# Attention: values stationary on halves of the array's columns, row sums from the exponentials, the second gate in four steps

## The chip, the cores and the metric

The program runs on one core of a Trainium2 chip. The metric is the device time of one execution in microseconds (us). The kernel before was timed three times: 1039.23 us in the median, from 1036.54 to 1039.69. Its engines, as the profile names them, are PE (TensorE, the matmuls; PEld is its weight loads), DVE (VectorE), ACT (ScalarE), POOL (GpSimd) and SP (the queue that issues most DMAs).

## What is computed

Three stages follow one another; each needs the whole result of the one before.

```python
# 1. attention: 2 batches, 8 heads, 576 rows, head size 64, a window of 128 keys
scores = where(0 <= rel < 128, q @ k.T / 8 + bias, -1e9)
attn   = exp(scores - max(scores));  attn /= attn.sum(-1) + 1e-9
x      = attn @ v                       # 1152 rows of 8 * 64 = 512
# 2. eight experts, each row goes to its best one (capacity 288)
e = argmax(x @ w_gate);  x = gate_w * (relu(x @ w1[e]) @ w2[e])
# 3. eight dense experts, mixed by a balanced matrix
P = exp(x @ w_gate2 - max);  8 times: rows, then columns of P to equal sums
out = sum over e of P[:, e] * (relu(x @ u1[e]) @ u2[e])
```

## The kernel before

**Attention.** The 576 rows of a batch are cut into blocks of at most 128, ten in all; blocks 4 and 9 have 64 rows. A unit is a block with four of the eight heads, so there are 20 units, and unit u belongs to block u // 2. A block looks at its own keys and at those of the block before it in its batch, so most units have two key parts, and the first block of a batch has one. Each unit passes through these steps:

- `scores` (PE, L444 and L437): the heads lie in pairs on the two halves of the array's rows (64 rows each).
- `pick` and `limit` (DVE, L453 and L470): mask, bias and the row's maximum; `powers` (ACT, L479): the exponential of one head at a time.
- `turn_p` (PE, L488) turns the probabilities, and `take_p` (ACT L501 and L508, POOL L509, DVE L506) copies them to `pT`, split by key part.
- `values` (PE, L532, and L522 for blocks of 64 rows): the turned probabilities are the stationary operand (128 columns), the values stream. `vb` holds 64 value columns and a column of ones for each head, so the row sum comes out as column 65. A matmul streams 128 columns (`WIDE`), more than the 65 that are used. In float32 each matmul is two records in the trace.
- `norm` (DVE, in three steps: L557, L559, L561, or L546, L548, L552 for 64 rows): row sum plus 1e-9, reciprocal, product into `x`. The result of `values` has a single PSUM bank (`xps`), so `values` of the next unit waits for the last step of `norm`.

When both units of a block are normed, `turn_x` (L569), `take_x`, `logits` (L583), `top`, `gate` and the counting steps choose each row's expert. Casts that split weights in two parts (`split_hi` on ACT L215, `split_lo` on POOL and DVE L222) are strewn in between.

The order of all this is written out by hand: the table `ORDER` names the steps, and the function `in_order` makes every engine run its instructions in that order. No engine overtakes in its own queue.

**First experts.** From about 108.6 us on, eight experts in turn: two layers in split precision (L772, L776).

**Second experts.** The first of the eight dense experts goes in three chunks of 384 rows (`j`). Into its layer 1 (L1301) and layer 2 (L1340) the steps of the list `sink` are mixed by `sink_next`: `gate_2` first, one step with three rounds of eight matmuls (L1074), a copy out of PSUM (`lsb`, DVE L1078), three transposes (L1081) and another copy (L1082); then eight rounds of row sums and column sums (the column sums with a matmul on PE, L1111). In this part the instructions are not in a table's order: the compile step places them, and token sums (`tsums`, L1184 to L1212) for the later experts stand among them. The other seven experts then run in passes with fewer products (L1383, L1414), up to the end.

Of the kernel before, what the change touches and what calls it, by code (L numbers as in the profile page):

```python
# [1 line left out]

# [7 lines left out]
F32 = mybir.dt.float32  # L10
# [19 lines left out]
take_q.0 load_block.2 scores.0 load_v.0 limit.0.1 turn_q.1 load_block.4 constants take_k.1 take_q.1 rest_k.1  # L30
limit.0.0 turn_k.2 turn_q.2 load_block.3 limit.0.1 load_weight.0 limit.0.0 more_constants powers.0.1 rest_q.1
powers.0.0 scores.1 turn_p.0.1 turn_p.0.0 take_k.2 limit.1.0 take_q.2 limit.1.0 scores.2 take_p.0.0 limit.1.1 sides
rest_q.2 zero_row powers.1.0 take_p.0.1 limit.1.1 pick.2.0 pick.2.1 values.0.0 turn_p.1.0 limit.2.0 values.0.1
rest_k.2 limit.2.0 turn_k.4 norm.0 take_k.4 limit.2.1 limit.2.1 powers.1.1 norm.0 turn_p.1.1 powers.2.0 scores.3
turn_p.2.0 rest_k.4 norm.0 turn_k.3 turn_q.3 pick.3.0 limit.3.0 limit.3.0 scores.4 load_v.1 powers.2.1 take_p.1.0
take_k.3 values.1.0 load_weight.1 pick.3.1 take_p.2.0 take_p.1.1 powers.3.0 limit.3.1 rest_k.3 turn_p.2.1 limit.3.1
split_hi.0 split_lo.0 split_hi.1 split_hi.2 values.1.1 split_hi.3 turn_q.4 pick.4.0 limit.4.0 split_lo.1 turn_p.3.0
split_lo.2 split_lo.3 limit.4.0 powers.4.0 norm.1 norm.1 scores.5 norm.1 take_p.2.1 pick.4.1 values.2.1 pick.5.1
take_p.3.0 load_weight.2 load_v.2 take_q.3 turn_x.0 limit.5.1 take_q.4 limit.4.1 rest_q.3 powers.3.1 load_block.5
take_x.0 values.2.0 load_weight.3 split_hi.4 limit.4.1 turn_p.3.1 norm.2 limit.5.1 split_lo.4 split_hi.5 pick.5.0  # L40
split_lo.5 norm.2 logits.0 split_hi.6 take_p.3.1 split_hi.7 turn_p.4.0 scores.6 top.0 norm.2 powers.5.1 limit.5.0
top.0 values.3.0 limit.5.0 pick.6.1 rest_q.4 take_p.4.0 split_hi.8 limit.6.1 pick.6.0 turn_p.5.1 values.3.1
limit.6.1 top.0 powers.4.1 norm.3 split_lo.6 turn_p.4.1 load_block.6 split_hi.9 split_hi.10 norm.3 scores.7
limit.6.0 split_hi.11 turn_k.5 norm.3 values.4.0 take_p.5.1 powers.5.0 turn_p.5.0 choice.0 pick.7.0 take_p.4.1
pick.7.1 limit.6.0 split_lo.7 values.4.1 limit.7.1 turn_q.5 gate.0 powers.6.1 take_p.5.0 turn_p.6.1 limit.7.1 norm.4
take_k.5 powers.6.0 take_q.5 scores.8 choice.0 norm.4 norm.4 turn_x.1 pick.8.0 take_p.6.1 limit.8.0 limit.7.0
limit.7.0 take_x.1 values.5.1 turn_p.6.0 load_v.3 values.5.0 turn_k.6 rows pick.8.1 limit.8.0 norm.5 logits.1
rest_k.5 take_k.6 top.1 count.0 norm.5 powers.7.0 take_p.6.0 norm.5 scores.9 pick.9.0 rest_k.6 powers.8.0 turn_x.2
# [41 lines left out]
def fused_kernel(ctx, tc, q, k, v, wg1, w1, w2, wg2, u1, u2, out, capacity):  # L90
# [157 lines left out]
    with ExitStack() as st:  # L248
# [225 lines left out]
        def powers(a):  # L474
# [3 lines left out]
            for a in range(2 * i, 2 * i + 2):  # L478
                nc.scalar.activation(pr[:n, a, :], sc[:n, a, :], AF.Exp, bias=nmx[:n, a:a + 1], scale=-1.0)  # L479
# [1000 lines left out]
```

## Time and profile before

| | |
|---|---|
| median of three runs | 1039.23 us |
| the profiled execution, its own time | 1038.18 us |
| its span from first to last instruction | 1036.1 us |
| PE busy over the span | 1018.7 us (98%) |
| DVE / ACT / POOL busy | 677.8 / 387.3 / 315.5 us |
| mean granted clock of PE, as a share of 2.4 GHz | 0.998 |
| attention, up to the first matmul of the experts | 0 to 108.6 us |
| first experts | 108.6 to 264 us |
| second experts | 264 to 1036 us |

A busy time counts an instruction from its start to its end. Matmuls are pipelined, so several are in flight at once; how long a group of them holds PE is read from the start of the group to the start of the next. A wait is idle time of an engine, put down to what ended it.

### The profile page before, as it was taken

Reading aid. Unit: us, or ns where it says so; the run is one execution under the profiler, and the core shown is the slowest. Engines: PE = TensorE matmul, PEld = TensorE weight load, DVE = VectorE, ACT = ScalarE, POOL = GpSimd, SP = SyncE. Lnnn points to the kernel's source line nnn. Section 1 sums busy time; section 2 is a strip of 40 time slices with the busy share of each in tenths; the row PEclk is TensorE's granted clock in tenths of the full one; section 3 lists DMA queues with packets and bytes.
Section 4 is the critical chain, followed back from the end, with each engine's and each line's share of the span. In section 5 each row is a group of like instructions: output and inputs, shape, how many; then the busy total and the mean of one; then the engine's idle time right before and its main releaser. Section 6 shows DMA issues by size and latency. Waiting matters only on the chain.

```text
span 1036.1 us, 16836 instructions
## 1 busy us (share of the span) xinstructions
PE 1018.7 (98%) x6388; PEld 930.3 (90%) x6388; DVE 677.8 (65%) x1644; ACT 387.3 (37%) x838; POOL 315.5 (30%) x305
## 2 busy tenths in 40 slices
PE   8999999999999999999999999999999999999997
PEld 6888999999889998999898999999898999999896
DVE  7988788778783347575756657575756657575752
ACT  6744477767321313232332323232322323232320
POOL 6533153341200123341313332241313332242113
PEclk9999999999999999999999999999999999999999
DMA  9931589986200112020211112020211112020102
GB/s 216 230 71 58 168 213 249 248 255 215 79 1 1 49 34 81 2 82 6 78 41 41 41 41 83 1 82 1 82 41 42 41 41 82 1 82 1 41 1 92
DMA packets 74103, 83.22 MB, mean 80 GB/s; under 512 B 31585, under 2 KB 45921, under 8 KB 74018
## 3 DMA queue, kind: packets, MB, share of 16 engines
q1 hardware_dynamic: 71906, 76.59, 25.0%
q0 software_dynamic: 2112, 5.52, 2.0%
q8 instruction: 51, 0.84, 0.3%
q14 instruction: 34, 0.28, 0.1%
HBM read 77.37 MB, written 4.73 MB: 79 GB/s over the span
## 4 chain that ended last, share of the span: by engine, by line
PE 72%; issue 2%; POOL 1%; DVE 1%; POOLq 0%; ACT 0%
PE pr L1414 31%; PE pr L1383 30%; PE ops L1340 5%; PE hps L1301 5%; PE pb L772 1%; POOL out_dram L1418 1%; PE pb L776 1%; PE lps L1074 0%; DVE tsums L1187 0%; POOL w_wlo L1278 0%; PE cps L1111 0%; POOLq L1476 0%; DVE lsb L1078 0%; DVE y_lo L1184 0%; PE ltp L1081 0%
## 5 line engine op out<-in xcount | busy, mean ns | idle before, releaser
L1414 PE MATMUL pr<-w_whi,hT 128*128 128x512 f32 x1008 | 315.8, 390 | 0.2 <-DVE hT L1375 0.2
L1414 PEld LDWEIGHTS pr<-w_whi,hT 128*128 128x128 f32 x1008 | 189.2, 188 | 39.5 <-DVE hT L1375 0.5
L1414 PE MATMUL pr<-w_wlo,hT 128*128 128x512 f32 x504 | 196.4, 390 | 0.0
L1278 POOL TENSOR_TENSOR w_wlo<-r,w_whi 128x512 fp32r<-128x512 f32 x56 | 71.4, 1294 | 290.4 <-ACT w_whi L1277 180.5
L1416 DVE SCALAR_TENSOR_TENSOR acc<-pr,Pm,acc 128x512 f32<-128x512 f32 x126 | 91.3, 745 | 89.0 <-PE pr L1414 88.7
L1374 ACT ACTIVATE hT<-pr 128x256 fp32r<-128x256 f32 (+1 forms) x168 | 69.0, 411 | 176.0 <-DVE pr L1391 176.0
L1375 DVE SCALAR_TENSOR_TENSOR hT<-pr,hT 128x256 fp32r<-128x256 f32 (+1 forms) x168 | 77.0, 458 | 80.1 <-ACT hT L1374 80.1
L1383 PE MATMUL pr<-y_hi,wy 128*128 128x320 f32 (+1 forms) x560 | 122.7, 297 | 0.0
L1414 PEld LDWEIGHTS pr<-w_wlo,hT 128*128 128x128 f32 x504 | 94.6, 188 | 19.5 <-POOL w_wlo L1278 0.5
L1383 PEld LDWEIGHTS pr<-y_hi,wy 128*128 128x128 f32 x560 | 93.8, 188 | 0.3 <-DVE hT L1375 0.3
L1271 POOL TENSOR_TENSOR wy<-r,wy 128x512 fp32r<-128x512 f32 x28 | 40.0, 1427 | 172.1 <-ACT wy L1270 172.1
L1383 PE MATMUL pr<-y_lo,wy 128*128 128x256 f32 (+1 forms) x280 | 83.3, 297 | 0.0
L191 DVE TENSOR_TENSOR wlo<-w,whi 128x1024 fp32r<-128x1024 f32 x66 | 80.7, 1225 | 3.1 <-issue 3.1
L179 ACT CAST whi<-w 128x1024 fp32r<-128x1024 f32 x66 | 69.1, 1051 | 19.5 <-DMA w<-in_moe_w_dram 15.3
L772 PE MATMUL pb<-h,whi 128*128 128x384 f32 x256 | 74.9, 361 | 0.4 <-DVE t L792 0.4
L772 PE MATMUL pb<-xt,whi 128*128 128x384 f32 x256 | 74.3, 362 | 0.6 <-PEq L946 0.3
L1277 ACT CAST w_whi<-r 128x512 fp32r<-128x512 f32 x56 | 33.1, 619 | 94.1 <-PE pr L1414 93.2
L1374 ACT ACTIVATE hT<-h 128x256 fp32r<-128x256 f32 (+1 forms) x56 | 24.9, 445 | 115.7 <-DVE h L1391 115.7
L1383 PE MATMUL pr<-y_hi,wx_wlo 128*128 128x256 f32 (+1 forms) x224 | 64.6, 288 | 0.0
L1383 PE MATMUL pr<-y_hi,wx_whi 128*128 128x256 f32 (+1 forms) x224 | 64.4, 288 | 0.0
L1383 PE MATMUL pr<-y_lo,wx_whi 128*128 128x256 f32 (+1 forms) x224 | 64.4, 287 | 0.0
L1255 POOL TENSOR_TENSOR sums<-r 128x512 f32<-128x512 f32 x28 | 37.0, 1324 | 80.8 <-DMA r<-in_moe_w_dram 45.6
(363 smaller groups left out, 2253.6 us busy)
## 6 DMA issues: line engine op xcount, KB each, us to landing
w<-in_moe_w_dram SPq DMA_DIRECT2D x36, 1024.0 KB, 6.9
r<-in_moe_w_dram SPq DMA_DIRECT2D x56, 512.0 KB, 3.9
kb<-in_k_dram SPq DMA_DIRECT2D x8, 256.0 KB, 4.0
qb<-in_q_dram SPq DMA_DIRECT2D x8, 256.0 KB, 4.7
vb<-in_v_dram SPq DMA_DIRECT2D x8, 256.0 KB, 6.9
xg_d<-xg SPq DMA_DIRECT2D x8, 256.0 KB, 2.3
kb<-in_k_dram SPq DMA_DIRECT2D x2, 128.0 KB, 4.1
qb<-in_q_dram SPq DMA_DIRECT2D x2, 128.0 KB, 3.6
```

The source lines that it names most:

```text
L179: nc.scalar.copy(his[i][:, sl, :], raws[i][:, sl, :])
L191: nc.vector.tensor_tensor(out=los[i][:, sl, :], in0=raws[i][:, sl, :], in1=his[i][:, sl, :].bitcast(F32), op=ALU.subtract)
L772: nc.tensor.matmul(ps[:, 0:2 * W], whi, x.rearrange("p r w -> p (r w)"), start=(m == 0), stop=(m == K - 1))
L1271: nc.gpsimd.tensor_tensor(out=wy[1][:, i], in0=x, in1=wy[0][:, i].bitcast(F32), op=ALU.subtract)
L1278: nc.gpsimd.tensor_tensor(out=w2p[1][:, k], in0=x, in1=w2p[0][:, k].bitcast(F32), op=ALU.subtract)
L1301: nc.tensor.matmul(hpss[f], a, bb[c][:, cols], start=(c == 0 and m == 0), stop=(c == ND - 1 and m == 2))
L1340: nc.tensor.matmul(ops, a[:, tcol], bb, start=(m == 0), stop=(m == 3 * NF - 1))
L1374: nc.scalar.activation(hi, src, AF.Relu)
L1375: nc.vector.scalar_tensor_tensor(out=lo, in0=src, scalar=0.0, in1=hi.bitcast(F32), op0=ALU.max, op1=ALU.subtract)
L1383: nc.tensor.matmul(ps, a[:, i, c, f], b, start=(c == 0 and m == 0), stop=(c == 1 and m == 2))
L1414: nc.tensor.matmul(ops, a[:, k, s * P:(s + 1) * P], b[:, k, :], start=(m == 0), stop=(m == 6 * QP - 1))
L1416: nc.vector.scalar_tensor_tensor(out=acc[s], in0=ops, scalar=Pm[:, s, e:e + 1], in1=acc[s], op0=ALU.mult, op1=ALU.add)
```

## The change

The diff touches three places.

1. **Attention.** The values of two heads are stationary, each on one half of the array's columns (64 columns, `tile_position=(0, j * D)`), and the turned probabilities stream through. The result is turned (head size on the partitions), so two steps are new: `take_v` copies it from PSUM on ACT, and `turn_v` turns it back on PE with two transposes, into the other half of the same bank. The row sums are no longer a 65th column: they come from `accum_out` of the exponentials, one more ACT instruction for each of the 80. Column of ones, padding to 128 columns and the special form for 64 rows are gone.
2. **Second gate.** One step with three rounds becomes four steps: matmuls of round 0; turn of round 0 and matmuls of round 1; turn of 1 and matmuls of 2; turn of 2 and the start of the balancing. The copy `lsb` goes from DVE to ACT; the copy after the turn and the final sum become one reduction on DVE.
3. **Second chunk of the first dense expert.** Each block of layer 1 is cut in two, with one step of `sink` between the halves.

```diff
@@ ORDER
-limit.9.0 limit.9.1 take_x.2 take_q.6 top.1 values.6.1 limit.8.1 turn_p.7.0 rest_q.6 gate.1 scores.10 choice.1
...
+values.6.1 limit.8.1 take_v.6 turn_p.7.0 rest_q.6 gate.1 scores.10 turn_v.6 choice.1 take_p.7.1 logits.2 load_weight.4
...
@@ load_v
-            vb[t] = la.tile([P, H, D + 1], F32, tag="vb", name=f"vb{t}", bufs=4)
-            nc.sync.dma_start(out=vb[t][:n, :, 0:D], in_=v[b, :, s:s + n, :].rearrange("h p d -> p h d"))
-            nc.gpsimd.memset(vb[t][:, :, D:D + 1], 1.0)
+            vb[t] = la.tile([P, H, D], F32, tag="vb", name=f"vb{t}", bufs=4)
+            nc.sync.dma_start(out=vb[t][:n], in_=v[b, :, s:s + n, :].rearrange("h p d -> p h d"))
@@ powers
-                nc.scalar.activation(pr[:n, a, :], sc[:n, a, :], AF.Exp, bias=nmx[:n, a:a + 1], scale=-1.0)
+                nc.scalar.activation(pr[:n, a, :], sc[:n, a, :], AF.Exp, bias=nmx[:n, a:a + 1], scale=-1.0,
+                                     accum_out=sums_of[u][:n, a:a + 1])
@@ values, and two new steps
-            for j in range(2):
-                h = head(g, i2, j)
-                at = h * (D + 1)
-                cols = min(WIDE, (H - h) * (D + 1))
-                for i, (tk, nk) in enumerate(kparts[t]):
-                    nc.tensor.matmul(xpd[u][:n, i2, j * (D + 1):j * (D + 1) + cols], pTd[u, i2][:nk, i, j, :n],
-                                     vb[tk].rearrange("p h d -> p (h d)")[:nk, at:at + cols],
-                                     start=(i == 0), stop=(i == len(kparts[t]) - 1))
+                xpd[u] = ps_x.tile([P, 4, P], F32, tag="xps", name="xps")
+            for i, (tk, nk) in enumerate(kparts[t]):
+                for j in range(2):
+                    nc.tensor.matmul(xpd[u][j * D:(j + 1) * D, i2, :n], vb[tk][:nk, head(g, i2, j), :],
+                                     pTd[u, i2][:nk, i, j, :n], start=(i == 0), stop=(i == len(kparts[t]) - 1),
+                                     tile_position=(0, j * D))
+
+        def take_v(u):
+            n = blocks[units[u][0]][2]
+            xvd[u] = wk.tile([P, 2, P], F32, tag="xv", name="xv", bufs=1)
+            nc.scalar.copy(xvd[u][:, :, :n], xpd[u][:, 0:2, :n])
+
+        def turn_v(u):
+            n = blocks[units[u][0]][2]
+            for i in range(2):
+                nc.tensor.transpose(xpd[u][:n, 2 + i, :], xvd[u][:, i, :n], ident)
@@ norm
-            nc.vector.tensor_scalar_add(rec[:n], xps[:, :, :, D:D + 1], EPS)
+            rec = sums_of[u]
+            nc.vector.tensor_scalar_add(rec[:n], rec[:n], EPS)
...
-                                    in0=xps[:, :, :, 0:D], in1=rec[:n].to_broadcast([n, 2, 2, D]), op=ALU.mult)
+                                    in0=xpd[u][:n, 2:4, :].rearrange("p i (j d) -> p i j d", j=2),
+                                    in1=rec[:n].rearrange("p (i j o) -> p i j o", i=2, o=1).to_broadcast([n, 2, 2, D]),
+                                    op=ALU.mult)
@@ gate_2, now called with j
-            lsb = tp.tile([P, CH], F32, tag="t1", name="lsb")[:2 * E]
-            nc.vector.tensor_copy(lsb, lps[:2 * E, :])
+        lsbs[j] = tp.tile([P, CH], F32, tag="t1", name="lsb")[:2 * E]
+        nc.scalar.copy(lsbs[j], lps[:2 * E, :])
+    def turn_2(j):
+        ltp = ps_k.tile([P, CH], F32, tag="pk", name="ltp")
+        for i in range(TPC):
+            nc.tensor.transpose(ltp[:, i * 2 * E:(i + 1) * 2 * E], lsbs[j][:, i * P:(i + 1) * P], ident[:2 * E, :2 * E])
+        nc.vector.tensor_reduce(out=lg2[:, j * TPC:(j + 1) * TPC],
+                                in_=ltp[:, :TPC * 2 * E].rearrange("p (s r e) -> p s e r", s=TPC, e=E), op=ALU.add, axis=AX.X)
-    sink = [gate_2, None, sinkhorn_start] + [sinkhorn_rows, None, sinkhorn_columns] * 8
+    sink = [partial(gate_2, 0), both_2(0), both_2(1), last_2, None, None] + [sinkhorn_rows, None, sinkhorn_columns] * 8
@@ second chunk of the first dense expert
+            if j == 1:
+                layer1(f, range(2))
+                sink_next()
             layer1(f, range(2, ND) if f in hpss else range(ND))
```

Three places show what moves. The first is PE at the change from block 3 to block 4; `sps` are scores, `ptp` turned probabilities, `xps` the bank of `values`, `xtp` the turned rows of a whole block. Before:

```order
L532 MATMUL xps<-vb_499,pT 128x128
L532 MATMUL xps<-vb_743,pT 128x128
L488 MATMUL ptp<-ident,pr 128x64 x4
L488 MATMUL ptp<-ident,pr 128x128 x2
L444 MATMUL sps<-kS,qT_829 128x256 x12
L569 MATMUL xtp<-ident,x 128x128 x4
L522 MATMUL xps<-vb_743,pT 128x130
```

Now, with `turn_v` as L534 and `values` as L521:

```order
L521 MATMUL xps<-pT,vb_503 64x128 x2
L521 MATMUL xps<-pT,vb_759 64x128 x2
L491 MATMUL ptp<-ident,pr 128x64 x4
L491 MATMUL ptp<-ident,pr 128x128 x2
L445 MATMUL sps<-kS,qT_848 128x256 x12
L534 MATMUL xps<-ident,xv 128x128 x2
L556 MATMUL xtp<-ident,x 128x128 x4
L521 MATMUL xps<-pT,vb_759 64x64 x2
```

The two new transposes stand right ahead of `xtp`, which reads the rows that DVE makes from them. The second place is ACT while the first weights are split (`whi`), in the third microsecond decade. Before:

```order
L479 ACTIVATE pr<-sc,nmx 128x128 x2
L575 COPY xT<-xtp 128x512
L215 CAST whi_529<-w_1_418 128x512 x4
L479 ACTIVATE pr<-sc,nmx 128x128 x2
L508 COPY pT<-ptp 128x256
L215 CAST whi_594<-w_2_497 128x512
```

Now, with `take_v` as L528:

```order
L481 ACTIVATE pr,rec<-sc,nmx 128x128 x2
L562 COPY xT<-xtp 128x512
L217 CAST whi_538<-w_1_420 128x512
L528 COPY xv<-xps 128x256
L217 CAST whi_538<-w_1_420 128x512 x3
L481 ACTIVATE pr,rec<-sc,nmx 128x128 x2
L508 COPY pT<-ptp 128x256
L217 CAST whi_601<-w_2_501 128x512
```

One copy is new between the casts, and each exponential now also writes a row sum (`rec`). The third place is the second gate's copy `lsb`. Before it was on DVE, here its third round among the token sums:

```order
L1184 TENSOR_TENSOR y_lo_1975<-tsums,y_hi_1971 128x256
L1187 TENSOR_TENSOR tsums<-y_hi_1973,y_lo_1977 128x256
L1187 TENSOR_TENSOR tsums<-y_hi_1972,y_lo_1976 128x256
L1078 COPY lsb<-lps 16x384
L1204 TENSOR_TENSOR tsums<-tsums 128x256
```

Now it is on ACT, with the second and the third round shown:

```order
L1314 ACTIVATE h__5673<-hps_5660 128x384
L1066 COPY lsb<-lps 16x384
L1183 CAST y_hi_2049<-tsums 128x256
L1183 CAST t_0_5592<-tsums 128x256
L1314 ACTIVATE h__5708<-hps_5695 128x384
L1183 CAST y_hi_2051<-tsums 128x256
L1066 COPY lsb<-lps 16x384
```

The third copy left a queue of token sums on DVE and stands behind three casts of token sums on ACT.

## Rows read from the trace of the kernel before

**Rows 1.** Busy time by stage: stage and length, then PE, PEld, DVE, ACT, POOL.
```profile
20.00:33.00 13.00, 12.02 (x108) 10.18 (x107) 11.05 (x52) 12.02 (x32) 11.51 (x12) 1.00 1.00 291
33.00:60.00 27.00, 25.41 (x231) 22.07 (x231) 24.29 (x143) 14.93 (x44) 9.26 (x15) 1.00 0.78 179
60.00:92.00 32.00, 31.20 (x318) 28.16 (x317) 30.22 (x173) 16.65 (x53) 12.86 (x16) 1.00 0.17 51
92.00:108.60 16.60, 16.14 (x120) 13.44 (x119) 12.86 (x74) 4.85 (x16) 3.20 (x4) 1.00 0.20 65
```
**Rows 2.** Waits of PE over the whole span: who for whom, us, times, longest.
```profile
PE ltp L1081 <- DVE lsb L1078: 2.1, 1, 2.1
...
PE xps L532 <- DVE x L561: 0.6, 2, 0.4
```
**Rows 3.** PE in order of time: start, us, line, operation, records.
```profile
52.71 1.65 PE L522 MATMUL xps<-vb,pT 128*128 128x130 f32 x8
54.29 0.44 PE L488 MATMUL ptp<-ident,pr 128*128 128x128 f32 x2
...
76.49 1.06 PE L532 MATMUL xps<-vb,pT 128*128 128x128 f32 x8
77.38 0.60 PE L569 MATMUL xtp<-ident,x 128*128 128x128 f32 x4
77.82 1.06 PE L532 MATMUL xps<-vb,pT 128*128 128x128 f32 x8
...
79.56 0.97 PE L444 MATMUL sps<-kS,qT 64*128 64x256 f32 x12
80.47 1.15 PE L583 MATMUL lgp<-wg_sb,xT 128*128 128x120 f32 x8
```
**Rows 4.** PE by line in attention: records, busy us, mean ns, idle before.
```profile
L532 PE MATMUL xps<-vb,pT 128*128 128x128 f32 (+1 forms) x224 | 31.1, 279 | 2.0 <-DVE pT L506 0.6 <-DVE x L561 0.6 <-PE sps L444 0.5
...
L522 PE MATMUL xps<-vb,pT 128*128 128x130 f32 (+1 forms) x32 | 6.8, 319 | 0.2 <-DVE x L552 0.2
```
**Rows 5.** Weight loads by shape: of 128 columns and of 64 columns.
```profile
L444 PEld LDWEIGHTS sps<-kS,qT 64*128 64x128 f32 x144 | 9.3, 185 | 2.0 <-issue 1.2 <-DVE rec L557 0.2 <-DVE nmx L470 0.2
...
L444 PEld LDWEIGHTS sps<-kS,qT 64*64 64x64 f32 x48 | 2.3, 131 | 0.2 <-DVE rec L557 0.2
```
**Rows 6.** ACT in order of time.
```profile
23.35 0.35 ACT L508 COPY pT<-ptp 128x256 f32<-128x256 f32 x1
...
31.75 0.21 ACT L607 ACTIVATION_READ_ACCUMULATOR ex<-lgp,ngm 128x1 f32 x1
31.84 0.70 ACT L479 ACTIVATE pr<-sc,nmx 128x128 f32<-128x128 f32 x2
```
**Rows 7.** DVE by line, the steps of norm: records, busy us, mean ns.
```profile
L561 DVE TENSOR_TENSOR x<-xps,rec 128x256 f32<-128x256 f32 x16 | 6.7, 416 | 0.3
...
L552 DVE TENSOR_TENSOR x<-xps,rec 64x128 f32<-64x128 f32 x8 | 2.3, 287 | 0.2
...
L546 DVE TENSOR_SCALAR rec<-xps 64x2 f32<-64x2 f32 x8 | 1.3, 158 | 3.6 <-PE xps L522 3.5
```
**Rows 8.** PE in order of time at the third turn of the second gate.
```profile
278.70 0.34 PE L1301 MATMUL hps<-y_hi,wlo 128*128 128x384 f32 x1
278.88 0.33 PE L1301 MATMUL hps<-y_hi,whi 128*128 128x384 f32 x1
281.30 0.35 PE L1081 MATMUL ltp<-ident,lsb 16*128 16x16 f32 x3 [2.08 <-DVE lsb L1078]
```
**Rows 9.** DVE in order of time at the same place.
```profile
277.87 2.92 DVE L1187 TENSOR_TENSOR tsums<-y_hi,y_lo 128x256 f32<-128x256 f32 x2
280.71 0.54 DVE L1078 COPY lsb<-lps 16x384 f32<-16x384 f32 x1
```
**Rows 10.** PE by single microseconds: busy, records, granted clock, DMA.
```profile
109.00:110.00 1.00, 1.00 (x8) 0.69 0.00 0
...
112.00:113.00 1.00, 1.00 (x7) 0.60 1.04 408
```

More of the change, by code (lines that the diff above doesn't have):

```diff
@@ L39 @@
[L39 to L48, printed above, removed]
@@ new lines @@
+take_v.5 turn_k.6 rows pick.8.1 limit.8.0 norm.5 logits.1 turn_v.5 rest_k.5 take_k.6 top.1 count.0 norm.5 powers.7.0
+take_p.6.0 norm.5 scores.9 pick.9.0 rest_k.6 powers.8.0 turn_x.2 pick.9.1 limit.9.0 limit.8.1 load_block.7 turn_q.6
+place.0 limit.9.1 powers.7.1 choice.0 top.1 turn_p.7.1 limit.9.0 limit.9.1 take_x.2 take_q.6 top.1 values.6.0
+values.6.1 limit.8.1 take_v.6 turn_p.7.0 rest_q.6 gate.1 scores.10 turn_v.6 choice.1 take_p.7.1 logits.2 load_weight.4
+norm.6 choice.1 load_v.5 limit.10.0 limit.10.0 load_v.4 count.1 limit.10.1 powers.9.1 scale_x.0 turn_q.7 limit.10.1
@@ new lines @@
+powers.8.1 norm.6 choice.1 place.1 scores.11 top.2 norm.6 limit.11.0 take_p.7.0 powers.9.0 top.2 powers.10.0 take_q.7
+turn_p.8.0 limit.11.1 limit.11.0 gate.2 load_block.9 rest_q.7 turn_p.8.1 turn_k.7 take_p.8.1 take_k.7 top.2 values.7.1
+values.7.0 norm.7 norm.7 scale_x.1 load_v.8 take_p.8.0 take_v.7 turn_p.9.0 turn_p.9.1 turn_p.10.0 take_p.9.0 scores.12
+turn_v.7 norm.7 powers.10.1 turn_x.3 values.8.1 values.8.0 take_v.8 turn_p.10.1 choice.2 take_p.9.1 take_x.3 pick.12.1
+logits.3 turn_v.8 limit.12.1 rest_k.7 mark.0 norm.8 norm.8 limit.11.1 norm.8 count.2 take_p.10.0 pick.12.0 top.3 top.3
@@ new lines @@
+limit.12.1 limit.12.0 table.0 add_table.0 place.2 values.9.0 values.9.1 powers.11.1 take_p.10.1 norm.9 choice.2
+limit.12.0 top.3 take_v.9 turn_p.11.1 powers.11.0 scores.13 turn_v.9 take_p.11.1 norm.9 norm.9 load_block.8 turn_x.4
+turn_p.11.0 mark.1 take_x.4 choice.2 choice.3 pick.13.0 gate.3 take_p.11.0 powers.12.1 values.10.0 values.10.1
+load_v.6 pick.13.1 limit.13.0 table.1 take_v.10 logits.4 turn_v.10 limit.13.0 norm.10 limit.13.1 count.3 add_table.1
+scale_x.2 turn_k.8 norm.10 norm.10 turn_p.12.1 powers.12.0 split_lo.8 limit.13.1 turn_p.12.0 values.11.1 values.11.0
@@ new lines @@
+place.3 take_k.8 norm.11 take_v.11 turn_q.8 mark.2 scores.14 turn_v.11 norm.11 top.4 norm.11 take_p.12.0 take_p.12.1
+choice.3 powers.13.0 powers.13.1 rest_k.8 pick.14.0 top.4 limit.14.0 choice.3 gate.4 take_q.8 load_v.7 pick.14.1
+table.2 limit.14.0 turn_p.13.1 top.4 values.12.0 values.12.1 mark.3 scale_x.3 powers.14.0 take_v.12 turn_q.9 rest_q.8
+norm.12 turn_p.13.0 add_table.2 scores.15 turn_v.12 norm.12 take_p.13.0 norm.12 take_p.13.1 turn_x.5 choice.4 take_x.5
+turn_p.14.0 values.13.0 values.13.1 limit.14.1 take_q.9 limit.14.1 pick.15.0 pick.15.1 take_v.13 logits.5 turn_v.13
@@ new lines @@
+rest_q.9 limit.15.1 limit.15.0 take_p.14.0 count.4 powers.14.1 table.3 turn_p.14.1 norm.13 limit.15.1 powers.15.1
+top.5 norm.13 scores.16 choice.4 place.4 top.5 norm.13 take_p.14.1 limit.15.0 choice.3 gate.5 top.5 choice.4 pick.16.0
+turn_p.15.1 scale_x.4 pick.16.1 take_p.15.1 turn_x.6 choice.5 limit.16.0 mark.4 values.14.1 values.14.0 load_v.9
+take_v.14 turn_k.9 powers.15.0 limit.16.0 limit.16.1 choice.5 take_x.6 powers.16.0 choice.1 limit.16.1 turn_p.15.0
+scores.17 turn_v.14 norm.14 add_table.3 choice.5 take_k.9 norm.14 logits.6 count.5 take_p.15.0 norm.14 pick.17.1
```

145 lines of the change are left out of this document (55 added, 90 removed).

## The prediction

> **What bounds the kernel now.** I read the table by stages first [rows 1], then the list of PE's waits, then PE in order of time, and only then single groups. From 108.6 us on, PE is busy without a break but for one wait of 2.1 us, in the second gate [rows 2], so there the change can give back that wait and little else. Attention is another matter. From 33 to 60 us PE is busy 25.4 of 27.0 us and DVE 24.3; from 60 to 92 PE 31.2 and DVE 30.2 of 32.0 [rows 1]. Two engines are full at once, and each runs a fixed order, so what PE is spared is worth no more than the gaps that DVE still has: 2.7 us in the one stage, 1.8 in the other. From 20 to 33 us it is ACT that is full, 12.0 of 13.0 us. From 92 on, PE is left alone with a chain that has little beside it. So the question is not how much shorter `values` gets, but where PE is the engine that the others wait for.
>
> **What `values` costs on PE.** A group of eight records of L532 holds PE from 76.49 to 77.38, 0.89 us; a group of L522, for 64 rows, from 52.71 to 54.29, 1.58 us [rows 3]. There are 28 groups of the first and 4 of the second (224 and 32 records [rows 4]): 24.9 + 6.3 = 31.2 us. A record of L532 so takes 0.111 us. A weight load of 128 columns lasts 0.185 us and one of 64 columns 0.131 [rows 5]: 64 columns cost 0.054, 128 cost 0.108. That is the 0.111, so today's record is bound by loading 128 columns of turned probabilities. With 64 value columns the load is 0.054.
>
> After, there are 224 + 64 = 288 records (the special form for 64 rows had half as many). No row shows a matmul on half of the columns; the nearest are the scores, on half of the rows. Twelve of their records hold PE from 79.56 to 80.47, 0.91 us [rows 3]. One after another, bound by their loads, they would take 12 x 0.108 = 1.30; as six pairs side by side 6 x 0.108 = 0.65. So they do run in pairs, and 0.26 us goes for changing from the whole array to its halves and back. For `values` this gives two ends: in pairs 288 x 0.054 / 2 = 7.8 us, one by one 15.6 us. If a record stays at 0.111 after all, it is 32 us and nothing is gained. I take the middle of the first two, 11.7 us. Twenty visits to the halves at 0.26 are 5.2 us. The 40 transposes of `turn_v` are like L569, four in 0.44 us (77.38 to 77.82 [rows 3]): 0.11 each, 4.4 us. Sum 21.3 against 31.2: PE is spared 9.9 us, from 6.0 to 13.8, or it pays 10 if the halves bring nothing.
>
> The Trainium skill has a rule against this change: "TensorEngine Tiling (Array Packing)", Key Properties, says that a change of tiling mode drains the engine. The 0.26 us around the scores agrees with it; by the rule the change pays that on every visit, as the sum has it, and without it the sum would be 5.2 us better.
>
> **What the new hop costs.** `values` of a unit now ends three engines later: PE, ACT (`take_v`), PE (`turn_v`), DVE (last step of `norm`), and only then is the bank free for the next unit and `x` ready for `turn_x`. Between `values` and `turn_v` the order has 1 us of PE work nearly everywhere (`turn_p` and the scores' 0.91 [rows 3], or logits), enough for the copy of 0.35 us [rows 6] if ACT is free. Behind `turn_v` it is otherwise. After the last transpose is issued come its 0.16 us in flight (0.60 against 0.44 [rows 3]), the product of 0.42 [rows 7] and two handoffs that I put at 0.1 each: 0.75 us. In seven places PE has next to nothing in between: ahead of `turn_x` of blocks 0, 3, 4, 8 and 9, and of `values` 16 and 19. I count 0.65 us each, and 0.2 in five places with some work: 5.6 us. The waits of `xps` on the product, 0.6 us in two places now [rows 2], are what these grow from. In the middle stages they cost only what PE could have gained. PE's net saving is 9.9 - 5.6 = 4.3 us, from 0.4 to 8.2.
>
> **ACT.** 80 reads of a row sum come in: a read begun at 31.75 lets the next exponential start at 31.84 [rows 6], so 0.09 each, 7.2 us, and 20 copies at 0.35, 7.0 us. From 33 us on ACT has idle time for that. From 20 to 33 it has 1.0 us left [rows 1] and gets 12 reads and four copies, 2.5 us: 1.5 too many, of which I charge 1.0 (0 to 2).
>
> **DVE and the rest.** The order of DVE is the same as before. A full unit costs it the same. A unit of 64 rows had two adds and two products, 2 x 0.158 + 2 x 0.287 = 0.89, and now has one of each, 0.158 + 0.416 = 0.57 [rows 7]: 0.3 us, four times, 1.3 us in the cover of PE and the tail. The memset of POOL and the padding in `vb` go; no engine waits for them. The load is the same bytes.
>
> **Attention by stage.** 20 to 33: +1.0. 33 to 60: seven and a half groups of L532 and two of L522 start here, a third of `values`, so 3.1 us of PE less 1.3 of new waits: -1.8, under DVE's gap of 2.7. 60 to 92: 14 groups, 4.0 us less 1.6 of waits, but DVE has 1.8 us of gap and much of that is not PE's: -0.8. From 92: two units of 64 rows at 1.58 become 0.9 (16 records at 0.04 and a change of mode), -1.3; three pairs of transposes +0.7; three of the seven waits at 0.65 in a chain with no cover, +1.9, less the 0.2 that L522 waits today [rows 4]: +1.1 (0 to 2). Sum -0.5, from -5 to +4.
>
> **The second gate.** PE waits 2.08 us at the third turn, up to 281.30, for a copy that DVE reaches at 280.71 behind two token sums of 2.92 us [rows 8, 9]. With four steps, 12 matmuls of layer 1 stand between each round's matmuls and its turn, at 0.18 each (278.70 to 278.88 [rows 8]) 2.2 us, and the copy on ACT I put at the 0.54 us of DVE's [rows 9]. The first two turns are free. The third copy on ACT stands behind casts that wait for the same token sums. Those end a little earlier, since DVE is rid of the copies (0.54 each [rows 9]); I put them at 280.4, and two casts, a relu and the copy, at an estimated 0.4 each, give 282.0. PE gets there with 14 matmuls more done, at 281.5. So about 0.6 us of the wait is left and 1.5 is gained (0.3 to 2.2). The halved blocks of the second chunk make the rounds of column sums come every 3.2 us of PE. DVE's short steps fit in barely; I cost it at nothing, cover being the 18 matmuls between two rounds. If that is too little, four rounds would hold PE for up to the 0.6 that `xps` waits show: 2.4 us at most.
>
> **The sum.** 1038.18 us, the profiled execution's own time, less 0.5 and 1.5: 1036.2. That execution lies 1.05 below the median of the runs shown, and I add half of it: 1036.7 us. A difference of 0.3% (3.1 us) is about what a measurement of this kernel can tell from none; 1036.7 is 2.5 below the median, inside it.
>
> **Rivals.**
>
> *The halves run in pairs and PE was the bound.* For it: the scores do run in pairs, and the list of waits has almost none of PE for DVE. Against it: DVE's 30.2 of 32. PE saves 13.8 - 5.6 = 8.2. The gaps of DVE cap it: 33 to 60 -3.3 (2.7 and the two short units), 60 to 92 -1.8, tail 0, ACT's stretch 0: -5.1. With -2.1 for the gate that is 1031.5. The Trainium skill, "TensorEngine Tiling (Array Packing)", Key Properties, says that different tiles can load and multiply in parallel; that is this rival's rule, and no row here shows it for columns. Chance 0.24.
>
> *The copy on ACT comes late (slower).* ACT runs in order, and `take_v` stands behind exponentials (two take 0.7 us [rows 6]), casts and copies that wait themselves. If it starts half a microsecond late, all twenty `turn_v` hold PE that long: +10 us. With PE's -4.3 that is +5.7, with -1.5 for the gate +4.2: 1042.9. It decides from a delay of about 0.25 us in the mean, where it eats PE's saving. Against it: ACT is busy only half of the time after 33 us. Chance 0.17.
>
> *The clock.* After the thin stretch from 92 to 108.6 the granted clock falls below its upper level of 2.4 GHz for four microseconds, to 0.69, 0.50, 0.50 and 0.60 (the first and the last of four rows stand in [rows 10]), 1.7 us lost. Shorter matmuls and new waits make PE's work thinner in attention as well. Two more such stretches: +3.4, 1040.1. Chance 0.06.
>
> *The gate's wait only moves.* The copy is still late, behind the casts: 0 instead of -1.5, 1038.2. Chance 0.06.
>
> **Chances.** Forecast 0.47, with a range of its own from 1033.5 to 1039.5; a third of that lies below 1036.1, where faster begins: 0.16, and 0.31 the same. First rival 0.24 faster. Second 0.12 slower, 0.05 the same. Clock and gate 0.12 the same. Together: faster 0.40, same 0.48, slower 0.12. For the range I go below the first rival (the gate whole and DVE's gaps whole) to 1030.5, and up to 1041.5, short of the second.
>
> **What would show it.** Groups of eight `values` records in about 0.4 us plus the change of mode; if they are 0.9 us, the halves bring nothing. Waits of PE behind the product at `turn_x` and `values` in the seven places. First matmul of the experts between 107 and 110 us: at 104 the first rival is right, beyond 111 the second. The wait at the third turn of the gate at 0.6 us or less. Waits of `xps` transposes for ACT of 0.5 us and more would make the forecast wrong, and so would new waits for column sums in the second chunk.

## The result and the profile after

The changed kernel takes 1051.41 us (median of 4 runs, 1045.35 to 1052.81) against 1037.88 for the kernel before beside it: a ratio of 1.0103, 95% interval 1.0067 to 1.0139. It is 13.5 us slower, and lies above the forecast range. The profiled execution took 1050.62 us, with a span of 1048.9.

The first expert product starts at 121.31 us, before at 108.61: attention is 12.7 us longer. The experts, from there to the first product of the dense stage (278.40, before 264.00), are 1.7 longer, and the dense stage is 1.6 shorter (770.5, before 772.1). So the loss is attention's; the other two stages cancel.

Its stages, with the columns of [rows 1]:

```profile
20.00:33.00 13.00, 11.27 (x120) 8.54 (x118) 10.86 (x56) 12.83 (x40) 12.17 (x11) 1.00 1.06 307
33.00:60.00 27.00, 23.44 (x216) 18.12 (x217) 20.09 (x114) 16.14 (x68) 8.03 (x10) 0.87 0.63 155
60.00:92.00 32.00, 28.80 (x298) 22.87 (x299) 25.14 (x153) 19.11 (x82) 9.35 (x11) 0.95 0.19 48
92.00:108.60 16.60, 14.46 (x136) 10.90 (x136) 10.79 (x64) 8.34 (x35) 7.16 (x8) 0.79 0.16 57
108.60:121.30 12.70, 11.53 (x102) 9.71 (x101) 9.31 (x57) 2.85 (x9) 1.04 (x1) 1.00 0.15 52
```

Compare with [rows 1]: from 60 to 92 us DVE fell from 30.2 busy microseconds to 25.1 and PE from 31.2 to 28.8, and behind 92 PE now has 26.0 us of work where it had 16.1. From 33 us on no engine is full any more; two engines that were nearly full now wait for each other. The granted clock, 1.00 throughout in the same rows of before, is 0.87, 0.95 and 0.79 in three stages. The waits of PE, who for whom, in us, times and longest, are short and scattered from 12 us to the end of attention, 11.4 us in all where the kernel before had 3.7 (here those over 1 us, and the gate's):

```profile
PE ptp L491 <- ACT pr L481: 2.5, 4, 0.9
PE ptp L491 <- DVE pT L506: 2.1, 4, 0.9
...
PE xtp L556 <- DVE pT L506: 1.3, 1, 1.3
PE xps L521 <- DVE x L546: 1.1, 2, 0.7
...
PE ltp L1071 <- DVE h__5708 L1315: 0.5, 1, 0.5
```

PE hardly waits at `turn_v` (L534): the list has no row of it, and the line's own view has 0.2 us, once. Those who wait are DVE, at the last step of `norm` (L546), and ACT, at `take_v` (L528). From 12 us to the first expert product:

```profile
DVE x L546 <- PE xps L534: 11.4, 10, 3.2
DVE x L546 <- ACT pr L481: 4.9, 3, 2.1
...
DVE x L546 <- PE lgp L630: 1.1, 1, 1.1
DVE x L546 <- ACT whi L217: 0.8, 1, 0.8
...
ACT xv L528 <- PE xps L521: 21.5, 13, 2.8
```

In all, DVE stands at L546 for 18.2 us. Before, `norm` waited 3.6 us at the first step of the short units and 0.3 at the product of the full ones [rows 7], and 1.1 at the first step of the full ones (L557). The 4.9 us put down to the exponentials belong to the transpose, I infer: the product needs nothing from ACT that the step ahead of it had not had. One unit of 64 rows shows how it comes about, in order of time, with PE, ACT and DVE:

```profile
63.30 1.12 PE L521 MATMUL xps<-pT,vb 128*64 128x64 f32 x16 [0.42 <-DVE x L546]
...
64.53 0.27 ACT L528 COPY xv<-xps 128x128 f32<-128x128 f32 x1 [1.62 <-PE xps L521]
...
64.72 0.98 PE L445 MATMUL sps<-kS,qT 64*128 64x256 f32 x12
...
65.63 0.41 PE L534 MATMUL xps<-ident,xv 128*64 128x128 f32 x2
...
66.14 0.42 DVE L546 TENSOR_TENSOR x<-xps,rec 64x256 f32<-64x256 f32 x1 [1.09 <-PE xps L534]
```

The copy is done at 64.80. The transpose starts at 65.63, because the scores are queued ahead of it on PE. DVE has nothing to do for 1.09 us, because all its next steps (here those that choose the rows' places, then picks and limits) are queued behind the product; and the exponentials that stand behind the copy on ACT start only at 64.69.

The clock fell after some of PE's gaps. PE by single microseconds (with the columns of [rows 1]), the granted clock again the third number from the end:

```profile
73.00:74.00 1.00, 0.15 (x2) 0.01 (x1) 0.75 (x3) 0.95 (x5) 0.00 (x0) 1.00 0.00 0
74.00:75.00 1.00, 0.62 (x9) 0.55 (x8) 1.00 (x4) 0.00 (x0) 0.97 (x1) 1.00 0.00 0
...
76.00:77.00 1.00, 0.89 (x12) 0.59 (x7) 1.00 (x9) 1.00 (x5) 0.60 (x1) 0.91 0.00 0
77.00:78.00 1.00, 1.00 (x8) 0.67 (x9) 1.00 (x2) 1.00 (x6) 0.44 (x1) 0.50 0.06 16
```

PE is idle for 1.2 us between 73 and 75, and from the end of 76 its clock is at the lower level (1.2 of 2.4 GHz) until 80. Two more such stretches lie around 39 to 46 and 97 to 104; the one of before behind the first expert products [rows 10] is gone. What they cost can be estimated from the four runs: three had a mean clock of 0.989 to 0.991 and took 1051.9 us in the mean, one had 0.998, as the kernel before, and took 1045.35. So, by that one run, about 6 of the 13.5 us go with the clock, and 7.5 are there without it. Why the clock fell after these gaps and not after others stays open (a gap as long kept it, in the run without the reads below). Of attention's 12.7 us that leaves some 7 for waits and transposes.

The gate's third turn, the answer to [rows 8], waits 0.48 us, as forecast; where the 1.6 us of the dense stage come from is another matter (the first experiment):

```profile
296.56 0.35 PE L1071 MATMUL ltp<-ident,lsb 16*128 16x16 f32 x3 [0.48 <-DVE h__5708 L1315]
```

### The profile page after: what moved, and what is told of

Same layout as the page of the kernel before. It is cut to its first block, busy times and chain, and to the rows that moved or that the text cites. A ratio compares the mean times of both kernels' runs of the same rounds, so it can differ in the third digit from the quotient of the medians.

```text
span 1048.9 us, 17066 instructions
## 1 busy us (share of the span) xinstructions
PE 1020.6 (97%) x6460; PEld 923.5 (88%) x6460; DVE 673.0 (64%) x1632; ACT 400.6 (38%) x941; POOL 318.9 (30%) x295
## 4 chain that ended last, share of the span: by engine, by line
PE 69%; DVE 2%; issue 2%; POOL 1%; POOLq 0%; ACT 0%; DVEq 0%
PE pr L1417 30%; PE pr L1386 29%; PE hps L1301 4%; PE ops L1343 4%; PE pb L759 1%; DVE tsums L1187 1%; POOL out_dram L1421 1%; PE pb L763 1%; POOL w_wlo L1278 0%; DVE tsums L1200 0%; DVE t_wlo L1184 0%; DVE tsums L1204 0%; PE lps L1062 0%; DVE t L1184 0%; DVE y_lo L1184 0%
## 5 line engine op out<-in xcount | busy, mean ns | idle before, releaser
L763 PE MATMUL pb<-h,wlo 128*128 128x192 f32 x256 | 60.4, 256 | 0.0
```

The source lines that it names most:

```text
L763: nc.tensor.matmul(ps[:, 0:W], wlo, x[:, 0, :], start=False, stop=False)
```

## The experiments

**The gate's part alone**, the kernel before with the part of the diff from `lsbs` on:

```
+    sink = [partial(gate_2, 0), both_2(0), both_2(1), last_2, None, None] + ...
```

> The kernel before with the gate's four steps and the second chunk's order alone; attention as before. In the changed kernel the attention took 12.7 us longer (first expert product at 121.31 us, before 108.61), the experts 1.7 longer and the dense stage 1.6 shorter. Theory (all the loss is in the attention, and the gate's part pays what was forecast): 1036.3 us, that is 1.6 below the kernel before's 1037.9, with the dense stage 1.6 shorter and attention and experts as before. Rival (the shorter dense stage was only a by-product of a later start, say of weights that had more time to land): 1037.9, dense stage as before.

Measured: 1036.52 us against 1038.23, ratio 0.9992 (0.9975 to 1.0009). By the times it can't be told from no change; in the trace attention and experts are as before (263.99) and the dense stage takes 770.5. The wait of 2.08 is 0.48, but a new one of 1.52 us for column sums stands behind it; from the list of PE in order of time:

```profile
282.14 0.35 PE L1085 MATMUL ltp<-ident,lsb 16*128 16x16 f32 x3 [0.48 <-DVE h__5630 L1329]
...
297.10 0.36 PE L1115 MATMUL cps<-cs,ones_f 128*128 128x8 f32 x2 [1.52 <-DVE cs L1109]
```

So PE waits 2.0 us here, as long as before, and the shorter third turn can't be the 1.6. The first product of the second dense expert, before and now, starts 109.15 and 108.83 us into the stage:

```profile
373.15 0.28 PE L1383 MATMUL pr<-y_hi,wx_whi 128*128 128x256 f32 x1
...
372.82 0.28 PE L1400 MATMUL pr<-y_hi,wx_whi 128*128 128x256 f32 x1
```

The first dense expert, in which the gate lies, gained 0.3 us, and the seven experts behind it 1.3, in small steps and with no wait of PE that went. All profiled runs with the gate's part whose clock stayed up in this stage have it at 770.5, so the gain comes with this edit; how it comes to the later experts is open.

**The row sums alone**, on the kernel before:

```
+                nc.scalar.activation(..., accum_out=sums_of[u][:n, a:a + 1])
-            nc.vector.tensor_scalar_add(rec[:n], xps[:, :, :, D:D + 1], EPS)
+            nc.vector.tensor_scalar_add(rec[:n], rec[:n], EPS)
```

> The kernel before with the row sums taken from the exponentials (80 accumulator reads on ACT) and used by the norm of the full blocks; the product keeps its column of ones, and no hop is added. Theory A (the hop through ACT and back is what costs; the reads fit into ACT's idle time): 1036 to 1040 us, attention within 1.5 us of before. Rival B (the reads make ACT late in every unit: 80 x 0.09 = 7.2 us): 1042 to 1045, first expert product at 113 or later, with new waits of PE for the exponentials.

Measured: 1041.04 us, ratio 1.0018 (1.0003 to 1.0032); in the profiled run the first expert product starts at 109.01, 0.4 later. The time lies between the two ranges. The attention decides for theory A: it is far from B's 113, and PE's list has no wait for the exponentials.

**The changed kernel without the reads:**

```
-                                     accum_out=sums_of[u][:n, a:a + 1])
-            nc.vector.tensor_scalar_add(rec[:n], rec[:n], EPS)
+            nc.vector.tensor_scalar(out=rec[:n], in0=ident[:n, 0:HG], scalar1=0.0, scalar2=1.0, op0=ALU.mult, op1=ALU.add)
```

> The changed kernel without the 80 accumulator reads: the exponentials give no sums, and the norm divides by a constant in instructions of the same number and shape, so the attention is not normalized. Theory A (the hop costs, not the reads): 1047 to 1051 us, DVE still waits some 15 us at the norm for the second transpose, and PE still loses its clock in the attention. Rival B (the reads): 1044 or less, PE's waits for the exponentials (2.5 us in four before) gone.

Measured: 1168.58 us, which tells nothing: with other values in attention the rows choose other experts, and the stages behind run longer (inferred from where the time lies). The expectations of this run and the next left that out. Read is only attention: first expert product at 115.70, with the clock at its upper level all the way and DVE's waits at the norm still 14.9 us. That is about what the changed kernel would have without its lost clock, 121.31 - 6 = 115. The reads are not the cause. And PE has a gap here as long as the one at 73 us above, after which the clock stays at its upper level (1.00 up to the end of attention):

```profile
71.00:72.00 1.00, 0.52 (x9) 0.37 (x7) 0.71 (x3) 0.63 (x2) 0.30 (x1) 1.00 0.00 0
72.00:73.00 1.00, 0.26 (x5) 0.20 (x3) 1.00 (x6) 0.00 (x0) 0.97 (x1) 1.00 0.00 0
```

**The changed kernel without the hop:**

```
-            nc.scalar.copy(xvd[u][:, :, :n], xpd[u][:, 0:2, :n])
-                nc.tensor.transpose(xpd[u][:n, 2 + i, :], xvd[u][:, i, :n], ident)
-                                    in0=xpd[u][:n, 2:4, :].rearrange(...)
+                                    in0=xpd[u][:n, 0:2, :].rearrange(...)
```

> The changed kernel without the hop: no copy on ACT and no second transpose; the norm reads the product as it lies, channels on the partitions, so each row gets values of the wrong place. The paired products and the accumulator reads stay. Theory A (the hop costs): 1030 to 1037 us, at or below the kernel before, first expert product at 102 to 108 us, DVE's wait at the norm under 5 us. Rival B (the reads cost): 1044 or more. Rival C (the clock falls because the paired product gives PE less to do, whatever the hop): half-clock stretches of 4 us or more stay in the attention before 100 us, and the time stays above 1040.

Measured: 1086.24 us, of which the same holds. The first expert product:

```profile
103.88 0.44 PE L757 MATMUL pb<-xt,whi 128*128 128x384 f32 x1 [0.25 <-DVE xt L239]
```

DVE's wait at the norm, the only one in its list:

```profile
DVE x L543 <- PE xps L521: 0.5, 1, 0.5
```

The stage from 60 us, as in [rows 1]:

```profile
60.00:92.00 32.00, 29.62 (x332) 23.04 (x331) 30.69 (x176) 20.43 (x86) 13.72 (x16) 1.00 0.21 63
```

The paired products with the reads end attention 4.7 us earlier than before; DVE hardly waits at the norm, is full again in the middle stage, and the clock stays up. So rival C falls and, for attention, theory A holds: the hop takes 17.4 us of the changed kernel's attention (some 6 of them with the clock), of which the 40 transposes themselves are 40 x 0.11 = 4.4.

**Attention alone**, the new attention with the old gate (the first experiment's complement):

```
-    sink = [partial(gate_2, 0), both_2(0), both_2(1), last_2, None, None] + ...
+    sink = [gate_2, None, sinkhorn_start] + ...
```

> The changed attention with the gate and the second chunk as in the kernel before; also a second sample of the attention's clock. Theory A (the two parts add up): 1.6 above the changed kernel, 1053.0 us where the attention loses its clock; the dense stage 772 us. Theory A2 (the half-clock stretches are a matter of chance in this attention, and cost 5 to 6 us): the runs fall into two groups by their mean clock, near 1053 at 0.99 and near 1047 at 0.998. Rival (the changed kernel's loss comes from the two parts together): 1040 or less.

Measured: 1052.80 us (1051.30 to 1056.77), ratio 1.0121 (1.0084 to 1.0158). That is 1.4 above the changed kernel, which fits theory A, but the intervals are too wide to tell 1.6 from none; the loss without the gate's part is shown. The dense stage took 773.7 us in the profiled run, with the clock at its lower level for some 3 us in it. The two groups of A2 did not show: the four runs had clocks of 0.986 to 0.993, so a mean clock of 0.998 (one run of four of the changed kernel) is not the rule in this attention.

**More work for PE**, one product per unit ahead of the second transpose:

```
+            nc.tensor.matmul(xpd[u][:, 2, :], ident, ident, start=True, stop=True)
```

> The changed kernel with one product more per unit on PE (two records of 128 columns, 0.22 us) that is written where the second transpose then writes; nothing reads it. 20 x 0.22 = 4.4 us of work for PE. Theory A (PE lost its clock because it waits and streams fewer columns; more columns keep the clock): the half-clock stretches between 38 and 104 us get shorter, 1046 to 1050 us. Rival (the clock doesn't depend on it, and PE's path is the end): 1054 to 1056.

Measured: 1051.80 us, first expert product at 126.20. Neither expectation fits. The clock fell in the profiled run as before (one of the four runs had 0.998, as in the changed kernel), so theory A's remedy fails. Two stages, with the granted clock as the third number from the end:

```profile
33.00:60.00 27.00, 23.42 (x214) 18.54 (x212) 19.28 (x111) 16.25 (x68) 7.91 (x10) 0.87 0.59 151
60.00:92.00 32.00, 28.90 (x279) 22.96 (x280) 23.13 (x137) 16.52 (x69) 7.83 (x8) 0.89 0.19 47
```

The product is queued right ahead of the transpose, behind work that PE did anyway; PE's busy time in these stages (23.4 and 28.9 us) is that of the changed kernel, so it did not fill the gaps.

**The second transpose one place earlier** in 18 units, ahead of the scores or logits; here of unit 1:

```
 turn_q.4 ... turn_p.3.0
+turn_v.1
 scores.5
-turn_v.1
```

> The changed kernel with the second transpose one place earlier on PE, ahead of the scores or logits (18 of 20 units), everything else in its order. Theory A (DVE's 18.2 us at the norm are there because the transpose stands behind a step of 1.0 us): DVE's wait at the norm falls to 8 us or less, PE waits at the transpose for the copy 0.1 to 0.3 us a unit, first expert product at 114 to 118, 1044 to 1048 us. Rival B (the hop's length counts, wherever it stands: product, copy, transpose, one after the other): PE's new waits at the transpose eat it, 1050 to 1054 us.

Measured: 1041.30 us, ratio 1.0025 (1.0008 to 1.0042). One move of two small transposes gives back 10.1 of 13.5 us, more than theory A had expected. Part of that is the clock: the one run of the changed kernel at 0.998 took 1045.35, and the four here at 0.998 and more 1040.1 to 1042.1, so some 4.6 us came back with the clock up. The same unit as above in order of time:

```profile
61.12 1.12 PE L521 MATMUL xps<-pT,vb 128*64 128x64 f32 x16
...
62.34 0.27 ACT L528 COPY xv<-xps 128x128 f32<-128x128 f32 x1 [0.91 <-PE xps L521]
...
62.66 0.41 PE L534 MATMUL xps<-ident,xv 128*64 128x128 f32 x2
...
63.00 0.97 PE L445 MATMUL sps<-kS,qT 64*128 64x256 f32 x12
63.17 0.42 DVE L546 TENSOR_TENSOR x<-xps,rec 64x256 f32<-64x256 f32 x1 [0.63 <-PE xps L534]
```

From the start of the product to the norm it is 2.05 us instead of 2.84. PE now waits for the copy, and DVE stands 9.8 us at the norm (with two single waits for others, 1.2 and 0.9) instead of 18.2. The first expert product starts at 115.08:

```profile
PE xps L534 <- ACT xv L528: 2.2, 5, 0.7
...
DVE x L546 <- PE xps L534: 7.7, 6, 2.4
...
115.08 0.44 PE L759 MATMUL pb<-xt,whi 128*128 128x384 f32 x1 [0.25 <-DVE xt L239]
```

**The norm's product later on DVE**, behind the picks, limits and masks that it held:

```
 scores.6 top.0
-norm.2
 powers.5.1 limit.5.0 top.0 limit.5.0 ... pick.6.0 turn_p.5.1
+norm.2
 values.3.0 values.3.1
```

> The changed kernel with the norm's multiplication later on DVE (18 of 20 units), as late as the single bank of the product and the block's own transpose allow, so that picks, limits and masks that were queued behind it go first. Theory A (DVE is held at the norm and with it the next unit's limits): DVE's wait at the norm falls from 18.2 to under 6 us; PE waits at the next product for the bank or at the block's transpose instead, some 0.4 us a unit, so 1044 to 1049 us. Rival B (the single bank is what holds): PE's new waits are as long as those that went, 1050 or more.

Measured: 1062.69 us, ratio 1.0211 (1.0172 to 1.0249). Rival B, and worse than it expected. DVE's wait at the norm fell to 9.7 us, not under 6, and PE's waits for it, up to 118 us, are about as long as what DVE was spared. The longest of PE's list (two more, at the same product and at `turn_x`, have 2.8 and 2.5):

```profile
PE xps L522 <- DVE x L547: 5.6, 8, 1.5
```

The product's single bank is free only behind the norm, so whoever moves the norm back holds the next product. The granted clock was 0.64 from 60 to 92 us, so part of the loss is again the clock's.

**No hop, but the product at the transpose's place.** The kernel before with row sums from the exponentials, and in its order, for 16 units:

```
-values.3.0
-values.3.1
 ...
 scores.7
+values.3.0 values.3.1
```

> No hop and no paired product: the kernel before with row sums from the exponentials (which alone came to 1041.0 us, attention 0.4 longer), and the product of 16 of the 20 units (not those of 64 rows) moved on PE to where the changed kernel has its second transpose, behind the scores or logits; DVE keeps its order. Theory A (what costs is that DVE stands at the norm for a PE step queued behind 1 us of other work, whatever that step is): DVE waits at the norm some 10 to 18 us, first expert product at 114 to 122 us, 1046 to 1056 us, with half-clock stretches. Rival B (the chain product, copy, transpose costs by its own length): 1040 to 1043 us, attention as in the run of the sums alone.

Measured: 1060.87 us, ratio 1.0205 (1.0170 to 1.0241), 20 us over the kernel with the sums alone. Its first expert product:

```profile
131.26 0.44 PE L773 MATMUL pb<-xt,whi 128*128 128x384 f32 x1 [0.25 <-DVE xt L236]
```

And DVE's wait at the norm's product:

```profile
DVE x L562 <- PE xps L533: 24.4, 12, 4.3
```

No copy, no second transpose, no halves: the same waits of DVE, the same lost clock (0.94, 0.95 and 0.90 in the three stages from 33 us), more time. That it is dearer than the changed kernel I put down to the length of what stands behind the scores, a product of 0.9 us (halves of a unit together 1.8) and not transposes of 0.2. With the run of the earlier transpose it points to the place, and not to the copy or the second transpose as such.

**One place more in six units** (of blocks 0, 2, 3, 6 and 7):

```
 turn_q.4
+turn_v.1
 turn_p.3.0
-turn_v.1
```

> The kernel with the second transpose one place earlier (1041.3 us), and in six more units another place earlier, with only one step of PE between product and transpose. Theory A: the remaining wait of DVE at the norm (9.8 us) falls a little, PE's waits for the copy rise by about 0.3 us in six units: 1039 to 1042 us. Rival B (the copy's latency now decides): 1043 or more.

Measured: 1042.68 us (1037.65 to 1045.62, 10 runs), ratio 1.0030 (1.0015 to 1.0044): no further gain. PE waits 3.5 us for the copy in six places. The ten runs go with their mean clocks, from 1037.65 at 1.000 to 1045.62 at 0.992, so here too the clock seems worth some microseconds. In the run with the full clock, the profiled one, the first expert product starts at 112.00; 103.88 and the 4.4 of the transposes would be 108.3. By that estimate, which lets PE pay every transpose in full, about 3.7 us of waits are left with the clock up, and a hop without any would stand where the kernel before stands, at 108.6.

**The product of before, cut to the 65 columns in use:**

```
-    WIDE = 128
+    WIDE = 65
```

> The kernel before with its product cut to the 65 columns that are used (values and ones; it streams 128, of which 63 are not read). Theory A (a record of 0.111 us is bound by loading 128 columns of weights): groups of eight stay at 0.89 us, the time within 3 us of before, 1036 to 1041, and the clock stays at its upper level up to 108 us, since PE has no more waits. Rival C (the clock falls when PE streams fewer columns, without any wait): half-clock stretches before 100 us and 1042 to 1048. Rival D (the record follows the streamed columns, and PE bounds): groups of 0.5 us, 1030 to 1034.

Measured: 1038.19 us against 1039.56, ratio 0.9988 (0.9969 to 1.0006). Groups of eight take 0.84 us (75.50 to 76.34), before 0.89 [rows 3]:

```profile
75.50 1.00 PE L532 MATMUL xps<-vb,pT 128*128 128x65 f32 x8
76.34 0.60 PE L569 MATMUL xtp<-ident,x 128*128 128x128 f32 x4
```

Theory A: half of the streamed columns save a twentieth, so the load of 128 columns, as sized in the prediction, is what bounds the record. Attention ends at 107.39 in the profiled run, 1.2 earlier. And the clock stays up through attention: PE with fewer columns and no new waits keeps it. Thinner work alone does not take the clock, here or without the hop. That the gaps do is argued, not shown: it fell only in runs with new waits, but the run without the reads had such gaps and kept it.

**Heads apart**, the two orders of the product's loops exchanged on the kernel with the earlier transpose:

```
-            for i, (tk, nk) in enumerate(kparts[t]):
-                for j in range(2):
+            for j in range(2):
+                for i, (tk, nk) in enumerate(kparts[t]):
```

> The kernel with the second transpose one place earlier, the products of a unit's half ordered head by head, so that neighbours in the order lie on the same half of the columns and not on the two halves. Theory A (the halves work side by side only in part, 0.064 us a record with the change of mode): a group of 16 records takes 1.3 to 1.8 us from start to start, not 1.02. Rival B (a record takes its own 0.054 to 0.064 us wherever the neighbour lies): still 1.0 to 1.1 us, and the pairing is worth nothing.

One run. A group of 16 and the record that follows it, here:

```profile
77.22 1.14 PE L521 MATMUL xps<-pT,vb 128*64 128x128 f32 x16
78.29 0.46 PE L377 MATMUL pt<-ident,qb 64*128 64x64 f32 x4
```

And the same group with the heads in turn, in the kernel with the earlier transpose:

```profile
72.56 1.09 PE L521 MATMUL xps<-pT,vb 128*64 128x128 f32 x16
73.59 0.46 PE L377 MATMUL pt<-ident,qb 64*128 64x64 f32 x4
```

1.07 against 1.03 us: rival B. The run's longer attention (120.52 against 115.08) has the clock at its lower level from 60 to 70 us; from one run I read nothing more.

**The two edits without the hop**, the gate's part and `WIDE = 65` on the kernel before:

> The gate's four steps and the second chunk's order on the kernel before, whose product streams the 65 columns in use: the two edits that were not slower by themselves (1.7 and 1.4 us under the kernel before run beside each), without the hop. Theory (they lie in different stages and add up): 1035.0 to 1036.5 us against some 1038.8, a ratio of 0.997, attention to 107.4 us, dense stage 770.5. Rival (each difference was the noise of its runs): ratio 0.999 to 1.001.

Measured: 1033.72 us against 1038.92, ratio 0.9956 (0.9940 to 0.9973): 5.2 us less, where the sum of the two alone was 3.1 (each of those was inside its noise). It beats both kernels. First products of the experts and of the dense stage:

```profile
107.88 0.44 PE L773 MATMUL pb<-xt,whi 128*128 128x384 f32 x1 [0.25 <-DVE xt L238]
...
261.11 0.33 PE L1315 MATMUL hps<-y_hi,whi 128*128 128x384 f32 x1
```

In the profiled runs attention is 0.7 us shorter, the dense stage 1.6 (770.5), and the experts 2.2 (153.2 against 155.4). The last was not expected, and the traces speak against crediting it to the edits: before lost 1.7 us there to its lower clock [rows 10] and PE stood idle for 0.7 us, this run lost no clock and 0.3; and the profiled run with the transpose another place earlier, which has neither the kernel before's attention nor `WIDE = 65`, has experts of 153.4.

## Why the prediction was wrong

**The step that failed is the price of the hop.** The prediction asked where PE waits behind `turn_v`, found seven places at 0.65 us and five at 0.2, and took 5.6 us off PE's saving. It asked of ACT how often it would be late, and of PE where it waits for what follows the norm. It never asked what DVE loses while it waits *for* `turn_v`: it noted that between product and transpose "the order has 1 us of PE work nearly everywhere", and counted that as cover for the copy. It is cover for the copy and delay for DVE. On DVE it said that the order is the same and a full unit costs the same; the first is true and the second nearly (all steps of `norm` 16.5 us busy, before 16.1), but the last step of the norm now stood there for a result 1 us later, in a queue where the next unit's limits come behind it. The runs put in its place: DVE held 18.2 us at the norm, in the end some 7 us of attention with the clock up and 6 more with the clock lost. The move of the transpose (10.1 us back, about half of it with the clock up) and the product at that place without any hop (20 us slower) show the place as the cause of the waits; why the clock fell with them stays open. (The 0.75 us behind the transpose is 0.78 by its own terms, which changes nothing.)

**What `values` costs** was sized nearly right, by a wrong split. From a group of 8 (0.58 us) and one of 16 (1.02 us) I estimate 0.055 us for a record and 0.14 for a visit to the halves: 288 x 0.055 + 20 x 0.14 = 18.6 us, where the prediction had 11.7 + 5.2 = 16.9. The two groups, each with the record that follows it, in the kernel with the earlier transpose:

```profile
64.52 0.66 PE L521 MATMUL xps<-pT,vb 128*64 128x128 f32 x8
65.10 0.21 PE L652 MATMUL tab<-zero_b,ones_b 128*96 128x24 bf16 x1
...
77.06 1.09 PE L521 MATMUL xps<-pT,vb 128*64 128x128 f32 x16
78.08 1.15 PE L570 MATMUL lgp<-wg_sb,xT 128*128 128x120 f32 x8
```

The records run one by one, at the end of 15.6 that it had named, and the visit costs half of what it took; 8 records in about 0.4 us, which were to show the middle, did not come. PE is spared 31.2 - 18.6 - 4.4 = 8.2 us, not 9.9. The Trainium skill, "TensorEngine Tiling (Array Packing)", Key Properties, says that different tiles can load and multiply in parallel; here neighbours on different halves save 0.04 us of 1.07.

**The first rival's -5.1 in attention** is near to what the kernel without the hop shows, -4.7, but by luck: that rival had the halves in pairs, the transposes and 5.6 us of waits in its sum, and this run has none of them. PE is spared 31.2 - 18.6 = 12.6 us there and attention gains 4.7, with DVE full again (30.7 of 32.0), which fits the prediction's cap by DVE's gaps. With the transposes' 4.4 on top, even a perfect order would, by this estimate, end about where the kernel before did.

**The second rival** had the sign and not the mechanism: it let PE wait for the copy, and PE waits 0.2 us at `turn_v` in all. Its mark, beyond 111 us, was met for another reason. **The clock** had 0.06 and 3.4 us as a case by itself; here it came in most runs, with the waits, at about 6.

**ACT's reads** were rightly small: 0.4 us of attention. **The gate** has the forecast's number, 1.6 gained, by luck. Its step was right, with 0.48 us of wait left at the third turn; but the new wait for column sums, costed at nothing and named as what would show the forecast wrong, is there once with 1.52 us and takes that gain back. Of the 1.6, the first dense expert has 0.3, and 1.3 come from the seven later ones, which the forecast left out.

Open is why the experts took 1.7 us longer in the profiled run. PE waited 2.6 us in three places behind DVE there (before 0.4, once), one of them (1.34 us at 208.09) behind a cast on ACT that waited for weights. No experiment was made on it.

## What to carry over

Where a result goes through another engine and back, look at three queues: what stands ahead of the second visit on the first engine, who waits for it, and what is queued behind the one that waits. Work put between the two visits to hide the copy is delay for whoever needs the result; put as much there as the copy takes, and no more. And when two engines are both full, a gap made on one comes back on the other; on TensorE the clock may fall as well, as it did here in most runs. A stage whose time comes out as forecast is still worth a second reading: the gate's did, for another reason.

## What the runs showed of the hardware

- On halves of the columns, with 64 stationary columns in float32, a record takes an estimated 0.055 us and a visit 0.14, and the two halves gain next to nothing from lying side by side (1.03 against 1.07 us for 16 records, one run).
- With 128 stationary columns, 65 instead of 128 streamed columns shorten a record from 0.111 to 0.105 us only.
- The granted clock fell to its level of 1.2 GHz after PE had been busy for 0.15 and 0.62 us in two successive microseconds (73 to 75 us of the changed kernel); it stayed at 2.4 GHz in another run after 0.52 and 0.26 us (71 to 73 us of the run without the reads). In the attention of the profiled runs it fell with and without the halves, only where there were new waits but not in all of them, and stayed up when PE streamed half of the columns without new waits.
